# A decode attention that loads the V of two heads as one transfer and runs its loops by pairs of heads

## The chip, the cores and the metric

The kernel runs on one core of a Trainium2 chip. The metric is the device time of one launch in microseconds (us). Before the change it is 2549.87 us, the median of three runs (2549.74 to 2549.97).

## The reference, cut to what matters

Two layers run one after the other; both use the same weights and the same caches. A layer is attention over a cache and then a small mixer with an MLP, for B = 2 sequences of one new token each, D = 576.

```python
def setup():
    B, Sq, D, H, Sk, Dh = 2, 1, 576, 32, 16384, 128
    k_cache, v_cache: (B, H, Sk, Dh) bf16
...
def _A_ref(x, k_cache, v_cache, wq, wo):
    q = (x @ wq) as heads                       # (B, H, 1, Dh)
    scores = einsum("bhqd,bhkd->bhqk", q, k_cache) * Dh ** -0.5
    p = softmax(scores)
    o = einsum("bhqk,bhkd->bhqd", p, v_cache)
    return o as (B, 1, H * Dh) @ wo
...
x = x + _A_ref(layernorm(x), ...)   # layer 0
x = x + _B_ref(layernorm(x), ...)   # w1, w2, w3 (576 x 4608), w4 (4608 x 576)
x = x + _A_ref(layernorm(x), ...)   # layer 1
x = x + _B_ref(layernorm(x), ...)
```

There are U = 2 x 32 = 64 heads a layer. K and V of one head are 16384 x 128 numbers of 2 bytes, 4 MiB each, so a layer reads 512 MiB of cache, and the DMA queue of the whole run moves 1092.40 MB (two heads and a part of a third are kept in memory between the layers).

## The kernel before, in words

**Memory and queue.** `mem` holds NSLOT = 6 slots of TILE = 32768 bytes a partition. One slot holds the K or the V of one head: 128 rows of 32768 bytes, partition p having the keys 128p to 128p + 127. Class `Store` (L269) keeps the list of all transfers of the program in a fixed order (`plan_all`, L499), each with its place in `mem`. A transfer is emitted by `pump` when every cell of its place has been given back by `release`; no later transfer overtakes it. All of them are issued by SP (L101) into one DMA queue, which the 16 DMA engines serve. `used` (L1229) counts what has been read of a tile and releases it after its last reader. `landed` (L1199) puts a relay on POOL, which tells PE, and in the loops DVE too, that a tile has come ("POOLq L202" in the profile).

**Order of tiles.** `tile_order` (L569) alternates K of head s and V of head s - 1. In layer 0 transfer i goes to slot i % 6, in layer 1 to slot (3, 4, 5, 0, 2, 1)[i % 6]. `order` (L565) gives the heads of a layer: 0 to 63 in layer 0, and 62, 63, 61, 0, 1, ..., 60 in layer 1, because the K and V of heads 62 and 63 and parts of head 61 stay in memory over the layers' boundary (CARRY = 2; `park` L1082, `turn`, `settle` and `carried` L1100 do their work there, partly with K already transposed). Head u is sequence u % 2, head u // 2 of it.

**One head** (`attention`, L954). Half of the 128 columns of keys go through PE, half through DVE.
- `q_broadcast` (L1208): DVE copies q's column (`q_col`) and makes `diag` = ident x q (L1213); PE multiplies ones by it (L1217), ACT copies the product (L1220): `qb` holds q in every row.
- PE's half: eight times `transposes` (L1246, 8 blocks of 128x128 into `tps`), `evacuate` by ACT (L1258, `kt`), `scores` (L1272, 8 products of one column into `sps`).
- DVE's half: four times `dots`, a multiply of 128x2048 (L1292) and a sum (L1296) into `s_dve`.
- `softmax_max` (L1299): DVE takes the maxima (L1307, L1310), POOL reduces over the partitions (L1312). `softmax_exp` (L1315): ACT scales (L1321) and takes the exp of both halves (L1324, L1327) into `p`, with the sums in `ls`.
- `pv` (L1348): 128 products of a V block by one column of `p` (L1366), gathered in `mps[:, 448]`. `keep_o` (L1332) and `keep_l` (L1337) store o and the sum on DVE.

Maximum, exp and PV of head s - 1 are interleaved with the transposes of head s: the maximum after its third chunk, the exp after its fifth, PV beside chunks 5 to 8.

**Loops.** PE, ACT and DVE each run real loops whose body holds NS = 3 heads: heads 2 to 61 in layer 0 and positions 4 to 63 of `order(1)` in layer 1, 20 turns each. The heads before and behind them are written out. Within a loop an operation has to have the same buffers in each turn.

**Between the layers.** Behind the loop `totals` (L1164) makes the sums' inverses, the wo, w3, w4 and wq products (L877) follow with weights that come through the same queue, in places that become free one by one. The column of o and l that belongs to a head is given by `place` (L1186); `home` (L1192) copies one column back after layer 1's loop.

Of the kernel before, what the change touches and what calls it, by code (L numbers as in the profile page):

```python
# [328 lines left out]
class KB:  # L329
# [13 lines left out]
    RAW = 2  # L343
    TURNS = {("w3", 0): 1, ("w3", 1): 1, ("w3", 2): 1, ("w4", 1): 1, ("w4", 3): 1, ("w4", 6): 1, ("w4", 8): 1,
# [27 lines left out]
    def _alloc(self):  # L372
# [6 lines left out]
        self.ident = sb("ident", [128, 128], BF16)  # L379
        self.ones_bf = sb("ones_bf", [128, 128], BF16)  # L380
        self.ones_f = sb("ones_f", [128, 128], FP32)
        self.diag = sb("diag", [128, 128], BF16)
        self.qb = [sb(f"qb{i}", [128, 128], BF16) for i in range(self.NS)]
        self.p = [sb(f"p{i}", [128, self.NB], BF16) for i in range(self.NS)]
# [5 lines left out]
        self.l = sb("l", [128, 1 + U], FP32)  # L390
        self.o_acc = sb("o_acc", [128, 1 + U], FP32)
# [15 lines left out]
        self.sel = [sb(f"sel{i}", [128, 128], BF16) for i in range(2)]  # L407
# [18 lines left out]
    def plan_tile(self, t, u, slot, cuts=(), skip=0):  # L426

        b, hh = u % self.B, u // self.B
        src = (self.K if t == "k" else self.V)[b, hh].rearrange("(p j) d -> p (j d)", p=128)
        cuts = [0, *cuts, self.NB]  # L430
        for a, z in zip(cuts[:-1], cuts[1:]):
            if a >= skip:
                self.plan_piece(t, u, slot * self.TILE, src, a, z - a)

# [64 lines left out]
    def plan_all(self):  # L499
# [8 lines left out]
        tiles = self.tile_order(0)  # L508
        place = [i % 6 for i in range(len(tiles))]
        place[-1] = 2  # L510
        half, quarter = self.BP, self.BP // 2
        for (t, u), slot in zip(tiles, place):
            self.plan_tile(t, u, slot, (half, half + quarter) if (t, u) == ("v", U - 1) else ())
        last = {tile: slot for tile, slot in zip(tiles, place)}
        third = U - self.CARRY - 1
        assert last["k", third] == 1 and last["v", third] == 4
# [19 lines left out]
        b, hh = third % self.B, third // self.B  # L536
        tiles = self.tile_order(1)
        b2, h2 = tiles[0][1] % self.B, tiles[0][1] // self.B
        for i in (1, 2, 3, None, 0):
            if i is None:  # L540
                self.plan_piece(*tiles[0], T, self.K[b2, h2].rearrange("(p j) d -> p (j d)", p=128), 0, quarter)
            else:
                self.plan_piece("v", third, 4 * T, self.V[b, hh].rearrange("(p j) d -> p (j d)", p=128),
                                i * self.GONE // 4, self.GONE // 4)
# [921 lines left out]
```

## Time and profile before

| what | value |
| --- | --- |
| median of three runs | 2549.87 us |
| the profiled execution | 2550.04 us |
| its span in the profile | 2548.1 us |
| mean granted clock of TensorE in it | 0.574 |
| instructions | 74895 |
| DVE busy | 1896.9 us |
| ACT busy | 1204.4 us |
| matmuls of PV (L1366) | 16384, 165 ns mean |
| multiplies and sums of DVE (L1292, L1296) | 504 each, 1224 and 2286 ns mean |

The profile is of one execution. Its span goes from the first to the last instruction; the device time of the same execution is 1.9 us longer. Engines are PE (TensorE products), PEld (TensorE weight loads), DVE (VectorE), ACT (ScalarE), POOL (GpSimd) and SP (SyncE, which issues the DMAs here). A row of the timeline gives start and length in us, engine, line, operation, output <- input, shape, and in brackets the idle time ahead of it with what ended it. In the slices of the span each digit is a busy share in tenths, where 9 is 90% or more. A row of DMA issues ends with the median time from issue to landing. "q1" is the queue that SP fills; its packets are single rows of the transfers and small packets of a few bytes.

### The profile page before, as it was taken

The page shows a single profiled execution, that of the slowest core. Times are in us where ns is not written, and L with a number is a line of the kernel's source. Part 1 is how long each engine was busy: PE and PEld are TensorE (multiplying, and loading weights), DVE is VectorE, ACT ScalarE, POOL GpSimd, SP SyncE. Part 2 cuts the span into 40 slices and gives each one's busy share as a digit, 9 for nine tenths or more (in the row PEclk, how much of TensorE's full clock was granted, in tenths as well). Part 3 has the DMA queues.
Part 4 walks back from the last instruction along what each step waited for, and adds up shares of the span by engine and source line. Part 5 has one row for each costly group of instructions (what it writes and reads, how often), then busy time and mean ns, then how long its engine had stood idle before and what let it go on. Part 6 is the DMA issues. An engine that isn't in the chain of part 4 may idle for free.

```text
span 2548.1 us, 74895 instructions
## 1 busy us (share of the span) xinstructions
PE 1614.3 (63%) x34407; PEld 1580.3 (62%) x34407; DVE 1896.9 (74%) x2061; ACT 1204.4 (47%) x1812; POOL 53.5 (2%) x151
## 2 busy tenths in 40 slices
PE   4666666656666666666767766666665666666566
PEld 3666666656665665666667756666665666666566
DVE  5877777777777777777638877777777777777774
ACT  3544544444454444445435544444454445444442
POOL 0000000000000000000000000000000000000000
PEclk8555555555555555555655555555555555555555
DMA  9999999999999999999999999999999999999999
GB/s 411 427 432 432 432 433 431 432 432 432 432 430 433 430 434 431 434 430 434 417 410 430 430 432 431 434 431 431 433 430 434 430 433 430 434 431 434 431 433 386
DMA packets 46928, 1093.19 MB, mean 429 GB/s; under 512 B 5140, under 2 KB 6296, under 8 KB 12440
## 3 DMA queue, kind: packets, MB, share of 16 engines
q1 hardware_dynamic: 46872, 1092.40, 100.0%
q8 instruction: 41, 0.67, 0.1%
q14 instruction: 15, 0.12, 0.0%
HBM read 1092.37 MB, written 0.00 MB: 429 GB/s over the span
## 4 chain that ended last, share of the span: by engine, by line
DMA 66%; DVE 23%; PE 5%; issue 5%; SPq 1%; ACT 0%; DVEq 0%; POOLq 0%
DMA mem<-in_A_k_cache_dram 63%; DVE s_dve L1296 12%; DVE prod L1292 9%; PE tps L1246 2%; PE mps L1366 2%; DMA mem<-in_B_w_dram 1%; DMA mem<-in_A_wo_dram 1%; PE sps L1272 1%; SPq L101 1%; PE sps L1217 1%; DVE diag L1213 0%; DMA mem<-in_A_wq_dram 0%; DVE l L1344 0%; DVE q_col L1210 0%; DVE mx L1307 0%
## 5 line engine op out<-in xcount | busy, mean ns | idle before, releaser
L1258 ACT ACTIVATE kt<-tps 128x1024 bf16<-128x1024 bf16 x992 | 1002.7, 1023 | 878.4 <-PE tps L1246 860.3
L1296 DVE TENSOR_REDUCE s_dve<-prod 128x16 f32<-128x2048 bf16 x504 | 1152.1, 2286 | 17.3
L1246 PE MATMUL tps<-ident,mem 128*128 128x128 bf16 x8192 | 999.4, 300 | 141.6 <-POOLq L202 135.2
L1292 DVE TENSOR_TENSOR prod<-mem,qb 128x2048 bf16<-128x2048 bf16 x504 | 616.8, 1224 | 525.0 <-POOLq L202 493.8
L1366 PE MATMUL mps<-p,mem 128*128 128x1 bf16 x16384 | 512.2, 165 | 549.9 <-POOLq L202 520.0
L1246 PEld LDWEIGHTS tps<-ident,mem 128*128 128x128 bf16 x8192 | 761.1, 136 | 151.6 <-POOLq L202 144.9
L1366 PEld LDWEIGHTS mps<-p,mem 128*128 128x128 bf16 x16384 | 487.6, 104 | 558.4 <-ACT p L1327 552.3
L1272 PEld LDWEIGHTS sps<-q_col,kt 128*128 128x128 bf16 x7936 | 399.1, 113 | 0.6 <-ACT kt L1258 0.5
L1272 PE MATMUL sps<-q_col,kt 128*128 128x1 bf16 x7936 | 387.6, 170 | 0.2
L1217 PE MATMUL sps<-diag,ones_bf 128*128 128x128 bf16 x127 | 36.4, 287 | 195.3 <-DVE diag L1213 195.3
L1217 PEld LDWEIGHTS sps<-diag,ones_bf 128*128 128x128 bf16 x127 | 13.2, 104 | 205.6 <-DVE diag L1213 205.6
L1321 ACT ACTIVATE mx<-mx 128x1 f32<-128x1 f32 x128 | 26.0, 203 | 235.9 <-POOL mx L1312 235.9
L1312 POOL PARTITION_ALL_REDUCE mx<-mx x128 | 51.1, 399 | 2442.2 <-DVE mx L1310 2323.5
L1220 ACT ACTIVATE qb<-sps 128x128 bf16<-128x128 f32 x127 | 35.2, 277 | 137.7 <-PE sps L1217 137.7
L1324 ACT ACTIVATE p<-s_dve,mx 128x64 bf16<-128x64 f32 x126 | 43.8, 348 | 4.1
L1258 ACT ACTIVATE mem<-tps 128x1024 bf16<-128x1024 bf16 x32 | 32.0, 1025 | 21.9 <-PE tps L1246 19.5
L1327 ACT ACTIVATE p<-sps,mx 128x64 bf16<-128x64 f32 x128 | 37.7, 294 | 0.1
L1307 DVE TENSOR_REDUCE mx<-sps 128x1 f32<-128x64 f32 x128 | 27.7, 216 | 7.3 <-PE sps L1272 7.2
L1213 DVE TENSOR_SCALAR diag<-ident,q_f 128x128 bf16<-128x128 bf16 x127 | 31.1, 245 | 0.0
L877 PE MATMUL mps<-prod,mem 128*128 128x2 bf16 x680 | 22.2, 166 | 14.1 <-DMA mem<-in_B_w_dram 8.3
L877 PEld LDWEIGHTS mps<-prod,mem 128*128 128x128 bf16 x680 | 20.6, 104 | 15.9 <-DMA mem<-in_B_w_dram 7.0
L710 ACT ACTIVATE misc<-misc 128x2 f32<-128x2 f32 x8 | 2.4, 296 | 51.8 <-DVE misc L708 51.8
(116 smaller groups left out, 293.7 us busy)
## 6 DMA issues: line engine op xcount, KB each, us to landing
mem<-in_A_k_cache_dram SPq DMA_DIRECT2D x124, 4096.0 KB, 40.7
mem<-in_A_v_cache_dram SPq DMA_DIRECT2D x123, 4096.0 KB, 49.6
mem<-in_B_w_dram SPq DMA_DIRECT2D x21, 576.0 KB, 7.8
mem<-in_B_w_dram SPq DMA_DIRECT2D x7, 1152.0 KB, 33.8
mem<-in_A_v_cache_dram SPq DMA_DIRECT2D x3, 2048.0 KB, 40.4
mem<-in_A_wq_dram SPq DMA_DIRECT2D x10, 512.0 KB, 6.6
mem<-in_A_wo_dram SPq DMA_DIRECT2D x8, 576.0 KB, 19.2
mem<-in_A_wq_dram SPq DMA_DIRECT2D x4, 1024.0 KB, 8.0
```

Source lines behind the costliest of these rows:

```text
L877: ins = pe.matmul(self.mps[:, t * B:(t + 1) * B], lhsT=buf[:, o:o + 128], rhs=rhs(k), start=(k == 0 and t == 0), stop=(k == last), skip_gr ...
L1217: self.pe(lambda pe: pe.matmul(qps, lhsT=self.ones_bf[:, :], rhs=self.diag[:, :], start=True, stop=True, skip_group_check=True), reads=["o ...
L1220: self.act(lambda e: e.activation(out=self.qb[i][:, :], in_=qps, func=ACT.Copy), reads=[("qps", i)], writes=[("qb", i)], sig=("qb", i))
L1246: ins = pe.transpose(self.tps[t][:, j * 128:(j + 1) * 128], buf[:, j * 128:(j + 1) * 128], self.ident[:, :])
L1258: self.act(lambda e: e.activation(out=out, in_=self.tps[t][:, :], func=ACT.Copy), reads=[("tps", t)], writes=keys, sig=("evac", c, t, k))
L1272: ins = pe.matmul(self.sps[sp][:, c * self.CH + j:c * self.CH + j + 1], lhsT=buf[:, j * 128:(j + 1) * 128], rhs=self.q_col[:, sp:sp + 1], ...
L1292: self.dv(lambda e: e.tensor_tensor(out=prod, in0=buf.rearrange("p (j d) -> p j d", d=128), in1=qbc, op=ALU.mult), reads=[("qb", r)] + key ...
L1296: self.dv(lambda e: e.tensor_reduce(out=sd[:, c0:c0 + DB], in_=prod, axis=AX.X, op=ALU.add), reads=["prod"], writes=[("s_dve", r)], sig=(" ...
L1312: self.pool(lambda e: e.partition_all_reduce(mx[3], mx[2], channels=128, reduce_op=ROP.max), reads=[("mx2", i)], writes=[("mx3", i)])
L1324: self.act(lambda e: e.activation(out=p[:, n:self.NB], in_=self.s_dve[i][:, 0:self.NB - n], func=ACT.Exp, bias=mx[4], scale=self.scale, ac ...
L1327: self.act(lambda e: e.activation(out=p[:, 0:n], in_=self.sps[i][:, 0:n], func=ACT.Exp, bias=mx[4], scale=self.scale, accum_out=self.ls[:, ...
L1366: ins = pe.matmul(self.mps[:, 448:449], lhsT=buf[:, j * 128:(j + 1) * 128], rhs=p[:, col:col + 1], start=b == 0, stop=b == self.NB - 1, sk ...
```

## The change

**V by pairs.** Head u now is sequence u // 32, head u % 32 of it, so that heads u and u + 1 lie one behind the other in the cache. In the loops the V of two heads comes as one transfer (`plan_pair`): 8 MiB as 128 rows of 65536 bytes over two slots. Partition p of it has the keys 256p to 256p + 255 of the two heads' 32768 together: the upper 64 partitions hold nothing but the second head, the lower 64 nothing but the first.

**Exp dealt out anew.** The exp of a head lies by K's layout, 128 keys in each of 128 partitions. For the pair, `spread_p` moves it by two products per head with a matrix of ones and zeros into 64 partitions (`both`), 256 columns. The matrix is a window with stride 2 on one tile that now holds ones, ident and the two `sel` matrices side by side (`same`). ACT copies the 64x256 part. `both` has two planes, one a head, and in each plane the other head's 64 partitions stay zero. `pv_pair` then makes 256 products with two columns, so that both heads' o come out at once, in `mps[:, 448:450]`; ACT stores them, and ACT stores the two sums (`keep_pair_l`).

**Loops by two.** A turn has two heads: transfers K, K, pair. The first head's maximum and exp stand in the second head, the second's stand at the end of the turn, with all scores drained before them. PV of both stands behind that. `q_broadcast` of the next head moves between the multiply and the sum of the last `dots` of a head. The loops go from position 1 to 61 (30 turns) in layer 0 and from 4 to 62 (29 turns) in layer 1. The head ahead of each loop is finished by itself first, its PV included; then DVE clears the upper half of `both`'s first plane.

**Places.** Layer 0: K0 in slot 1, V0 in 3, then K in 0 and 2 and the pair in 4 and 5; at the end K61 in 1, K62 in 3, V61 in 4, K63 in 5, V62 in 0, V63 in 2. Layer 1: the rest of its first fresh K in slot 3, its V in 5, then K in 0 and 4 and the pair in 1 and 2; at the end two K in 3 and 5, two V in 0 and 4. The first V after a layer's entry is planned ahead of the second K. The places of layer 1's wo, w3, w4 and w1 change with it.

**Small things.** `ones_f` is one column that is read with stride 0. The sums and o have no extra column, so `home` is gone, and the last product of spread, o and sums is one instruction instead of two.

The diff, cut to its core:

```diff
+    ENTER = (1, 4)
+    LEAVE = (61, 62)
...
-        self.ident = sb("ident", [128, 128], BF16)
-        self.ones_bf = sb("ones_bf", [128, 128], BF16)
+        self.same = sb("same", [128, 4, 128], BF16)
+        self.ones_bf, self.ident, *self.sel = (self.same[:, i, :] for i in range(4))
...
+        both = sb("both", [128, 4 * self.NB], BF16)
+        self.both = both[:, :].rearrange("p (k c) -> p k c", k=2)
...
+    def plan_pair(self, u, slot):
+        v = self.V.rearrange("b h s d -> (b h s d)")
+        n = self.NB * 128 * 128
+        self.store.plan(("w", u, 0, 2 * self.NB), "pair", slot * self.TILE, 2 * self.TILE,
+                        [(lambda m: m, v[u * n:(u + 2) * n].rearrange("(p x) -> p x", p=128))])
...
+        self.plan_tile("k", 0, 1)
+        self.plan_tile("v", 0, 3)
+        for u in range(1, third, 2):
+            self.plan_tile("k", u, 0)
+            self.plan_tile("k", u + 1, 2)
+            self.plan_pair(u, 4)
+        for t, u, slot in (("k", third, 1), ("k", third + 1, 3), ("v", third, 4), ("k", third + 2, 5),
+                           ("v", third + 1, 0), ("v", third + 2, 2)):
...
+        self.plan_tile("k", first, 3, (quarter, half, half + quarter), quarter)
+        self.plan_tile("v", first, 5)
+        for s in range(a, z, 2):
+            self.plan_tile("k", o[s], 0)
+            self.plan_tile("k", o[s + 1], 4)
+            self.plan_pair(o[s], 1)
+        self.plan_tile("k", o[z], 3)
+        self.plan_tile("k", o[z + 1], 5)
+        self.plan_tile("v", o[z], 0)
+        self.plan_tile("v", o[z + 1], 4, (half,))
...
+                                   inside=(lambda: self.q_broadcast(o[s + 1], s + 1)) if turning and c == 2 * n - 2 else None)
...
+                    if odd and c == LEAD:
+                        self.softmax_max(l, s - 1, o[s - 1])
+                    if odd and c == n:
+                        self.softmax_exp(l, s - 1, o[s - 1])
+                        self.spread_p(l, s - 1, 0)
...
+            if turning:
+                if odd:
+                    while pend:
+                        self.scores(*pend.pop(0))
+                    self.softmax_max(l, s, u)
+                    self.softmax_exp(l, s, u)
+                    self.spread_p(l, s, 1)
+                    self.keep_pair_l(l, s - 1)
+                    self.keep_pair_l(l, s)
+                    self.g.relay("tensor", ...)
+                    self.pv_pair(l, s - 1, o[s - 1])
+            elif s == enter - 1:
+                while pend:
+                    self.scores(*pend.pop(0))
+                self.softmax_max(l, s, u)
+                if s - 1 >= 0:
+                    self.keep_o(l, s - 1)
+                    self.keep_l(l, s - 1)
+                self.softmax_exp(l, s, u)
+                self.landed(l, "v", u)
+                for g in range(4):
+                    self.pv(l, s, u, g)
+                self.keep_o(l, s)
+                self.keep_l(l, s)
+                self.dv(lambda e: e.memset(self.both[64:, 0, :], 0.0), writes=self.both_keys)
...
+    def spread_p(self, l, s, k):
+        out = self.sps[0][:, 2 * k * n:2 * (k + 1) * n]
...
+            for h in range(2):
+                at = (1 - k) * 128 + h
+                lhsT = bass.AP(tensor=c.tensor, offset=c.offset + at, ap=[list(c.ap[0]), [2, 128]])
+                ins = pe.matmul(out[:, h * n:(h + 1) * n], lhsT=lhsT, rhs=self.p[i][:, :], start=True, stop=True,
+                                skip_group_check=True)
...
+        lo, hi = 64 * k, 64 * (k + 1)
+        self.act(lambda e: e.activation(out=self.both[lo:hi, k, :], in_=out[lo:hi, :], func=ACT.Copy), ...)
...
+    def pv_pair(self, l, s, u):
...
+                    ins = pe.matmul(self.mps[:, 448:450], lhsT=buf[:, b * 128:(b + 1) * 128], rhs=self.both[:, :, col],
+                                    start=b == 0, stop=b == 2 * self.NB - 1, skip_group_check=True)
...
+        self.act(lambda e, c: e.activation(out=self.o_acc[:, bass.ds(c, 2)], in_=self.mps[:, 448:450], func=ACT.Copy), ...)
+        self.used(l, nm, 2 * self.NB)
```

More of the change, by code (lines that the diff above doesn't have):

```diff
@@ L506, in plan_all @@
         self.plan_small("w2", 0, self.w2, 4 * T + wqr * n + wqr // 2, (0, 64))
-        tiles = self.tile_order(0)
-        place = [i % 6 for i in range(len(tiles))]
-        place[-1] = 2
         half, quarter = self.BP, self.BP // 2
-        for (t, u), slot in zip(tiles, place):
+        third = U - self.CARRY - 1
+        self.plan_tile("k", 0, 1)
[6 more added lines that the diff above has]
+                           ("v", third + 1, 0), ("v", third + 2, 2)):
             self.plan_tile(t, u, slot, (half, half + quarter) if (t, u) == ("v", U - 1) else ())
-        last = {tile: slot for tile, slot in zip(tiles, place)}
-        third = U - self.CARRY - 1
-        assert last["k", third] == 1 and last["v", third] == 4
         self.cuts = {}
```

205 lines of the change are left out of this document (114 added, 91 removed).

## The prediction

> **What bounds the kernel now.** I read the page first: busy shares, the slices, the queue, the chain.
>
> ```profile
> span 2548.1 us, 74895 instructions
> PE 1614.3 (63%) x34407; PEld 1580.3 (62%) x34407; DVE 1896.9 (74%) x2061; ACT 1204.4 (47%) x1812; POOL 53.5 (2%) x151
> ...
> DMA  9999999999999999999999999999999999999999
> GB/s 411 427 432 432 432 433 431 432 432 432 432 430 433 430 434 431 434 430 434 417 410 430 430 432 431 434 431 431 433 430 434 430 433 430 434 431 434 431 433 386
> ...
> q1 hardware_dynamic: 46872, 1092.40, 100.0%
> ...
> DMA 66%; DVE 23%; PE 5%; issue 5%; SPq 1%; ACT 0%; DVEq 0%; POOLq 0%
> ...
> mem<-in_A_k_cache_dram SPq DMA_DIRECT2D x124, 4096.0 KB, 40.7
> mem<-in_A_v_cache_dram SPq DMA_DIRECT2D x123, 4096.0 KB, 49.6
> ```
>
> No engine is busy for more than 74% of the span, while the DMA engines are busy in every slice, at about 432 GB/s wherever K and V stream. A 4 MiB tile is issued 40 to 50 us before it lands, so about four tiles stand in the queue at any time. The time is therefore bytes over rate, plus any moment in which the queue runs dry; there is none now but the ends. An engine's work counts only through the moment at which it frees a slot. So I ask two things: does a byte get cheaper, and does the queue still always hold something? For the second I took the timeline of a steady head.
>
> ```profile
> 617.51 0.25 DVE L1213 TENSOR_SCALAR diag<-ident,q_f 128x128 bf16<-128x128 bf16 x1
> 617.81 0.10 PEld L1217 LDWEIGHTS sps<-diag,ones_bf 128*128 128x128 bf16 x1 [1.58 <-DVE diag L1213]
> ...
> 618.14 0.28 ACT L1220 ACTIVATE qb<-sps 128x128 bf16<-128x128 f32 x1 [0.96 <-PE sps L1217]
> ...
> 622.12 1.22 DVE L1292 TENSOR_TENSOR prod<-mem,qb 128x2048 bf16<-128x2048 bf16 x1 [4.37 <-POOLq L202]
> ...
> 625.70 1.22 DVE L1292 TENSOR_TENSOR prod<-mem,qb 128x2048 bf16<-128x2048 bf16 x1
> ...
> 629.54 0.16 DVE L1310 TENSOR_TENSOR mx<-mx 128x1 f32<-128x1 f32 x1
> ...
> 629.79 0.35 POOL L1312 PARTITION_ALL_REDUCE mx<-mx  x1 [19.08 <-DVE mx L1310]
> ...
> 631.73 0.94 PEld L1366 LDWEIGHTS mps<-p,mem 128*128 128x128 bf16 x32 [5.13 <-ACT p L1327]
> ```
>
> Columns are start, length, engine, line, operation; in brackets the idle time and what ended it. DVE starts at 622.12 after 4.37 us of waiting for a tile: it has slack. A product and its sum take 625.70 - 622.12 = 3.58 us, four of them 14.32. From the last maximum (629.54) over POOL and three ACT steps to the first PV weight load (631.73) it is 2.19 us.
>
> **The change part by part.**
>
> **1. Rows of 65536 bytes.** Two stretches of the DMA view, one of K and V alone, one of weights in long rows:
>
> ```profile
> DMA packets 8599, 250.50 MB, mean 432 GB/s; under 512 B 953, under 2 KB 953, under 8 KB 953
> ...
> q1 hardware_dynamic: 8597, 250.48, 100.4%
> ```
>
> ```profile
> DMA packets 499, 5.11 MB, mean 426 GB/s; under 512 B 59, under 2 KB 59, under 8 KB 59
> ...
> q1 hardware_dynamic: 498, 5.09, 100.4%
> ```
>
> First stretch: 8597 packets of q1, of which 953 are the small ones, so 7644 rows of 32768 bytes (250.48 MB / 7644). In 580 us on 16 engines that is 1214.0 ns a row. A tile is 8 such rows an engine: 9.71 us. Second: 498 - 59 = 439 rows in 12 us, 437.4 ns for 11595 bytes on average. Two points give 0.03668 ns a byte and a fixed 12.1 ns a row. The two layers' loops hold 30 + 29 = 59 pairs; each pair makes 8 rows an engine out of 16. Saving: 59 x 8 x 12.1 ns = **5.7 us**. Ends: 0, if each long row is cut in two again; 8.3 us if the fixed part is 17.6 ns, which the weights stage (below) gives.
>
> ```profile
> DMA packets 5102, 19.85 MB, mean 397 GB/s; under 512 B 569, under 2 KB 569, under 8 KB 5084
> ...
> q1 hardware_dynamic: 5094, 19.73, 100.0%
> ```
>
> Here 5094 - 569 = 4525 rows took 50 us: 176.8 ns for 4360 bytes, and with the 1214.0 this gives 17.6 ns. I take 12.1, from the rows nearest in size. The Trainium skill ("DMA: Bandwidth & Descriptors", section "Where 436 GB/s comes from") puts the ceiling at 435.2 GB/s; by it the fixed part would be 9.3 ns, the saving an estimated 4.4 us and the sum 2562.
>
> **2. A turn of two heads.** Now slots decide. Before, six slots rotate. After, a loop uses four: one for each K, two for the V pair; two stand empty. Let D be the moment at which DVE starts on the first K of a turn. Other durations:
>
> ```profile
> 1253.90 3.57 PE L1366 MATMUL mps<-p,mem 128*128 128x1 bf16 x128 [0.50 <-ACT p L1327]
> ```
>
> ```profile
> 2546.57 0.29 SPq L101 DMA_DIRECT2D out_dram<-prod  x1
> ```
>
> A PV product in a long row of them costs 3.57 / 128 = 27.9 ns. A second column in it I cost at nothing: the weight load sets the pace. An issue needs under 1.5 us to land 2.2 KB (2546.57 to the span's end at 2548.1), so I take 1.4 us to the first byte.
>
> Even head: 14.32 + 0.4 (q_col and diag) = 14.7. Odd head: two products (7.16), the even head's maxima (0.4 by 629.54 + 0.16 against 625.70 + 3.58, taken as 0.5), the third product (3.58), the fourth multiply (1.26), q_col and diag (0.4): PE's q product at D + 27.6. Then last transposes, evacuation, scores, maxima: 3.1 us (next fence: q product 42.23, the first of six evacuations from 43.42 ends at 44.5, then scores and a maximum). Maximum at D + 30.7. The 2.19 us to PE, plus what the new deal of exp adds: two products (0.33, as from 617.81 to its evacuation), an ACT copy of 64x256 (I estimate 0.4, between 0.28 for 128x128 at 618.14 and 1.05 for 128x1024 in the next fence), two semaphores: 1.1. PV starts at D + 34.0, ends 256 x 27.9 ns later at D + 41.1; ACT's copy of two columns, SP's wait: 0.8; first byte of the next pair at **D + 43.3**. In the queue behind this K stand a K, a pair, two K: 5 x 9.71 = 48.55 us after its landing. D is 0.25 us after the landing, so 5.0 us are left. The second K's slot comes free at D + 28.9, first byte D + 30.5, wanted at 38.85: 8 us left. So in steady state the queue does not run dry; the new waits of PE (on exp, on the copy) hold up the next head's transposes behind them, but PE starts that head 3 us late and waits for DVE's diag until D + 12.4 anyway. Cost 0. DVE even loses work (keep_o and keep_l go to ACT). What it costs when this cover is gone stands under the rivals.
>
> **3. Loop entries.** In place of a head that flows into the loop there is now a head that is finished alone: scores drained, maxima, exp, 128 PV products, o and l kept, the memset, and only behind these on DVE the first product of the loop. Layer 0:
>
> ```profile
> 6.86 2.93 SPq L101 DMA_DIRECT2D mem<-in_A_v_cache_dram  x1
> ...
> 42.23 0.10 PEld L1217 LDWEIGHTS sps<-diag,ones_bf 128*128 128x128 bf16 x1 [8.46 <-DVE diag L1213]
> ...
> 43.42 6.31 ACT L1258 ACTIVATE kt<-tps 128x1024 bf16<-128x1024 bf16 x6 [0.58 <-PE tps L1246]
> ...
> 50.70 1.24 POOL L1312 PARTITION_ALL_REDUCE mx<-mx  x1 [35.54 <-DVE mx L1310]
> ...
> 61.52 1.23 DVE L1292 TENSOR_TENSOR prod<-mem,qb 128x2048 bf16<-128x2048 bf16 x1 [3.70 <-issue]
> ```
>
> ```profile
> mem<-in_A_v_cache_dram SPq DMA_DIRECT2D x1, 4096.0 KB, 40.2
> ```
>
> The queue starts K0, V0, K1, K2, all at once as before; the third tile lands at 6.86 + 40.2 = 47.1. The q product at 42.23, maximum at 45.3, 2.19 and 0.9 more because POOL's reduction takes 1.24 here instead of 0.35: PV 48.4 to 52.0; o, l, memset 0.7: 52.7. Then "issue" gaps: 3.70 at this very entry now. I take 2: D = 54.7. The next pair's first byte at 98.0 is wanted at 47.1 + 48.55 = 95.6: **2.4 us** dry (0.4 without a gap, 4.1 with 3.7).
>
> Layer 1:
>
> ```profile
> 1335.22 0.33 SPq L101 DMA_DIRECT2D mem<-in_A_v_cache_dram  x1
> ...
> 1343.05 1.36 POOL L1312 PARTITION_ALL_REDUCE mx<-mx  x1 [17.05 <-DVE mx L1310]
> ...
> 1349.90 1.84 PE L1366 MATMUL mps<-p,mem 128*128 128x1 bf16 x64
> ...
> 1357.60 0.10 PEld L1217 LDWEIGHTS sps<-diag,ones_bf 128*128 128x128 bf16 x1 [2.57 <-DVE diag L1213]
> ...
> 1360.57 0.77 PEld L1246 LDWEIGHTS tps<-ident,mem 128*128 128x128 bf16 x8 [1.71 <-issue]
> ```
>
> ```profile
> mem<-in_A_v_cache_dram SPq DMA_DIRECT2D x1, 4096.0 KB, 15.2
> ```
>
> Behind the rest of K0 come V0 and K1 (before: K1 and V0). The second of them, issued when V62's slot is free, lands at 1335.22 + 15.2 = 1350.4. Then K2, which now goes to slot 4, where V61 lies; its last PV ends at 1349.90 + 1.84 = 1351.7, first byte 1353.3: 2.9 dry. Before, K2 went to the slot of V63, whose PV is done before V61's. The lone head: q product 1357.60, maximum 1360.7, PV 1363.8 (reduction 1.36) to 1367.3, the rest 0.7, gaps 2 (1.71 at this entry now): D = 1370.0, where K1 landed 19.6 us ago. K3's slot is free at D + 13.5, byte 1385.1, wanted at 1382.4: 2.7. K4: D + 30.5 = 1400.5, wanted 1394.8: 5.7. Next pair: D + 43.3 = 1413.3, wanted 1410.2: 3.1. Sum **14.4 us** (12.4 without a gap, 17 with two). One turn later DVE is free before its tile lands again and the 5 us are back.
>
> **4. The rest at nothing.** At either layer's end K61, K62 (K59, K60) now land back to back, which shifts the last maximum by about 1.5 us.
>
> ```profile
> 1258.91 0.16 DVE L1310 TENSOR_TENSOR mx<-mx 128x1 f32<-128x1 f32 x1
> ...
> 1266.18 0.61 PEld L877 LDWEIGHTS mps<-prod,mem 128*128 128x128 bf16 x20 [0.39 <-DMA mem<-in_A_wo_dram]
> ```
>
> ```profile
> 2507.86 0.16 DVE L1310 TENSOR_TENSOR mx<-mx 128x1 f32<-128x1 f32 x1
> ...
> 2519.03 1.41 PEld L877 LDWEIGHTS mps<-prod,mem 128*128 128x128 bf16 x50 [0.68 <-DMA mem<-in_A_wo_dram]
> ```
>
> Behind both maxima the wo products already wait for their DMA (0.39, 0.68), so most hides; 0 to 2.8 us for the two if not. The changed order of q, o and l, the missing copies and one product fewer are under 1 us of DVE.
>
> **Sum.** -5.7 + 2.4 + 14.4 = +11.1 on the profiled run's 2550.04 (span 2548.1 and 1.9 around it); the median, 2549.87, is 0.17 less. **2561 us.**
>
> **Rivals.**
> - *The queue stays fed at the entries* (ends on the other side). Place: the two lone heads. If DVE reached the loop some 14 us sooner in layer 1 than I work out and K2's slot were free in time, only the long rows would count: 2544. It decides from D under 1355.6, where 43.3 us lead to 1398.9. For it: every slice is at full rate today. Against: the multiply-and-sum rows of one head alone run until 1357. Half of the loss gone, 2553, is within 0.2%.
> - *The row is cut again*: no gain, 2567. The packet count decides. Nothing in the trace speaks either way.
> - *The chain of a turn is longer than 5 us over my sum*: strided weights, a slow copy, gaps at each back edge. From D + 48.3 on each further us costs half a us in each of 59 turns (a pair's delay comes back every second turn): 2 us over give 2561 + 59 = 2620. Against: each step has its row, and the rows of a steady head show no such gap.
> - *Long rows move slower.* Their starts lie 64 KiB apart instead of 32. Were the pairs' 495 MB to go at the weights stage's 397 GB/s instead of 432, it would be +101: 2662. No row hints at it. The Trainium skill ("DMA: Bandwidth & Descriptors", section "Latency and other measured facts") has row pitches of large powers of two slow down, but first at 512 KiB; no run here shows it.
>
> **How the numbers follow.** Forecast 0.70, the cut row 0.13, the long chain 0.05, slow rows 0.02, fed entries 0.05, half of the loss 0.05. A measurement of this kernel can tell about 0.2% (5.1 us) from no change. Slower by more than that: 0.70 + 0.13 + 0.05 + 0.02, less 0.03 for the forecast's own lower edge, 0.87; same 0.05 + 0.03 = 0.08; faster 0.05. Range: the forecast's own ends are -8.3 + 0.4 + 12.4 = +4.5 (2554) and 0 + 4.1 + 17 + 2.8 = +23.9 (2574), the cut row lies inside; 2 us more on either side take in part of the half case and one more gap: 2552 to 2576.
>
> **What would show it.** q1 packets 46872 - 59 x 144 = 38376 (45928 if cut). DMA share under 1 around 1350 to 1415, and a little near 96; full elsewhere. K's median from issue to landing falls from 40.7 to between 20 and 26, and still nothing waits in the loops except DVE for a tile. I am wrong if the loops show DMA below 432, or if DVE begins layer 1's loop before 1360.

## The result, and the profile after

The changed kernel takes 2565.85 us (median of four runs, 2564.69 to 2569.81) against 2549.89 before: a ratio of 1.0065, with an interval of 1.0048 to 1.0083. It is slower by 16.0 us; 11.1 were forecast, in a range of 2552 to 2576. The profiled execution is the longest of the four, 2569.81 us with a span of 2567.9, so the stages below add up to 19.8 us and not to 16.0.

First the page of the changed kernel: span, slices, queue, the chain's shares, and the rows of K's DMA issues.

```profile
span 2567.9 us, 75499 instructions
PE 1590.8 (62%) x34642; PEld 1525.9 (59%) x34642; DVE 1876.3 (73%) x1821; ACT 1251.0 (49%) x2106; POOL 106.3 (4%) x152
...
DMA  9999999999999999999998999999999999999999
GB/s 413 382 435 438 426 440 425 433 434 431 433 438 426 432 435 429 432 436 429 398 401 362 410 426 432 432 440 425 440 426 432 433 436 427 439 427 433 435 430 394
...
q1 hardware_dynamic: 38376, 1092.39, 99.1%
...
DMA 59%; DVE 26%; PE 7%; issue 6%; ACT 1%; SPq 0%; POOL 0%; POOLq 0%; DVEq 0%; ACTq 0%
...
mem<-in_A_k_cache_dram SPq DMA_DIRECT2D x124, 4096.0 KB, 23.2
```

No engine is much busier than before, and the same bytes come in 38376 packets: the long rows are moved whole. The loss is in three places of the GB/s row: slice 2 (382), slices 20 and 21 (398, 401, where the kernel before has 417 and 410) and slices 22 and 23 (362, 410). K's issue to landing fell from 40.7 to 23.2 us. The queue that held about four tiles now holds two or three (23.2 us at 9.7 us a tile), so a slot that comes free late is felt sooner.

How much each stage costs can be read from the bytes. The next fences give what q1 has moved up to 140, 1180, 1340, 1500 and 2500 us, first before, then after (packets, MB, share of 16 engines).

```profile
q1 hardware_dynamic: 3149, 58.63, 98.7%
...
q1 hardware_dynamic: 18565, 507.69, 100.1%
...
q1 hardware_dynamic: 26565, 574.18, 100.1%
...
q1 hardware_dynamic: 28917, 642.83, 100.1%
...
q1 hardware_dynamic: 43812, 1074.41, 100.2%
```

```profile
q1 hardware_dynamic: 2761, 55.88, 94.7%
...
q1 hardware_dynamic: 14332, 505.82, 99.6%
...
q1 hardware_dynamic: 22119, 570.54, 99.5%
...
q1 hardware_dynamic: 23813, 632.90, 98.6%
...
q1 hardware_dynamic: 34938, 1065.58, 99.3%
```

The difference of two such rows over 0.432 MB a us is how far the changed kernel is behind at that moment: 2.75 MB at 140 us are 6.4 us. Rows that are on their way make an error of about 1 us, an estimate: 16 rows of 32768 bytes, one on each engine, are 1.2 us at this rate.

| stage | forecast, us | behind at its end, us | its own share, us |
| --- | --- | --- | --- |
| start and entry, layer 0 (to 140) | +2.4 | 6.4 | +6.4 |
| loop, layer 0 (to 1180) | -2.9 | 4.3 | -2.0 |
| layers' boundary (to 1340) | 0 | 8.4 | +4.1 |
| entry, layer 1 (to 1500) | +14.4 | 23.0 | +14.6 |
| loop, layer 1 (to 2500) | -2.8 | 20.4 | -2.5 |
| end | 0 | 19.8 (span) | -0.6 |

The two loop forecasts are the 5.7 us by their 30 and 29 pairs. Layer 1's entry and the loops came out near their forecasts; layer 0's entry and the layers' boundary were taken too small.

This execution is also worse than most in just these two. The second experiment below has the same kernel up to 1340 us, and its profiled execution took 2565.86 us, which is the median of the change. It is 4.5 us behind at 140 us, 2.9 at 1180 and 4.9 at 1340, so layer 0's entry and the boundary cost 4.5 and 2.1 us there instead of 6.4 and 4.1. The fourth experiment's profile gives 4.5 and 2.3.

A steady turn first, from the timeline of the changed kernel: DVE's first product of two turns running, and SP's issue of the next pair.

```profile
597.93 1.23 DVE L1344 TENSOR_TENSOR prod<-mem,qb 128x2048 bf16<-128x2048 bf16 x1 [8.60 <-POOLq L202]
...
636.71 1.23 DVE L1344 TENSOR_TENSOR prod<-mem,qb 128x2048 bf16<-128x2048 bf16 x1 [8.74 <-POOLq L202]
...
637.64 0.33 SPq L101 DMA_DIRECT2D mem<-in_A_v_cache_dram  x1
```

A turn takes 38.8 us, four tiles at 9.7. DVE stands 8.7 us of it for its tile, and the pair's slot is free at D + 39.7 (D: DVE's start on a turn's first K) where the prediction had D + 41.9 (its first byte at D + 43.3). Nothing is dry here. Now the entry of layer 0:

```profile
50.59 0.17 DVE L1077 MEMSET both<- 64x128 uint32 x1
...
57.39 1.23 DVE L1344 TENSOR_TENSOR prod<-mem,qb 128x2048 bf16<-128x2048 bf16 x1 [6.64 <-issue]
...
99.03 0.33 PE L1439 MATMUL mps<-both,mem 128*128 128x2 bf16 x7 [2.30 <-issue]
...
99.67 0.33 SPq L101 DMA_DIRECT2D mem<-in_A_v_cache_dram  x1
```

DVE is done with the lone head at 50.76 and begins the loop at 57.39: 6.64 us in which it waits for nothing that the profile shows ("issue"). PE stands 2.30 us in the same way within the first turn's PV. In the profiles of experiments 1, 2 and 4, with the same entry, these gaps are 5.43 to 5.54 and 1.61 to 1.79 us, which is about the 1.9 us by which their entry is cheaper. The queue's view of the same moments has the packets of the instruction queues, once from 50 to 58 us and once from 96 to 99.5:

```profile
q1 hardware_dynamic: 99, 3.60, 106.0%
q8 instruction: 1, 0.02, 0.9%
q14 instruction: 3, 0.02, 0.8%
```

```profile
q1 hardware_dynamic: 31, 0.49, 33.6%
q8 instruction: 1, 0.02, 1.7%
```

Ten packets of the instruction queues lie between 50 and 140 us, and only 3 in the 1040 us of the loop behind them, so code is loaded mostly there. But four of the ten lie between 58 and 96 us, where the timeline shows no such gap. The Trainium skill ("Runtime: NRT & Kernel Launch", section "Instruction fetch mechanics") says that an engine's code comes in pages over a DMA queue of its own and that a taken branch to a page that isn't there stalls the engine. The rows agree in place, with 6.64 and 2.30 us; that it is the cause was not isolated by a run.

Layer 1's entry (the second of the two transfers from 1341.27 on is K2):

```profile
1341.27 20.17 SPq L101 DMA_DIRECT2D mem<-in_A_k_cache_dram  x2
...
1359.24 1.84 PE L1465 MATMUL mps<-p,mem 128*128 128x1 bf16 x64
1361.48 0.43 SPq L101 DMA_DIRECT2D mem<-in_A_v_cache_dram  x1
...
1375.86 1.23 DVE L1344 TENSOR_TENSOR prod<-mem,qb 128x2048 bf16<-128x2048 bf16 x1 [0.26 <-issue]
...
1379.87 2.48 PEld L1294 LDWEIGHTS tps<-same,mem 128*128 128x128 bf16 x24 [4.85 <-issue]
...
1388.99 15.64 SPq L101 DMA_DIRECT2D mem<-in_A_k_cache_dram  x2
...
1418.02 0.33 PE L1439 MATMUL mps<-both,mem 128*128 128x2 bf16 x7 [2.83 <-issue]
...
1418.66 0.33 SPq L101 DMA_DIRECT2D mem<-in_A_v_cache_dram  x1
```

V61's last PV ends at 1361.08; only then does K2 go out, and the pair at once behind it. DVE begins the loop at 1375.86. 1370.0 was forecast on the clock of before; the changed kernel enters this stage 8.4 us behind that, so D is 2.5 us earlier than forecast, about the 2 us of gap that are 0.26 here. The next pair goes out 42.8 us later. The slices of 1340 to 1440 us show the dry places, one digit for each 2.5 us:

```profile
DMA  9999993065999999999969996099990919999996
```

They lie around 1355 to 1365, 1400 to 1405 and 1415 to 1422 us: in front of K2, of K4 and of the next pair. In front of K3, for which 2.7 us were forecast, one digit falls to 6 (1390 to 1392.5 us), which is about 1 us.

### The profile page after: what moved, and what is told of

Read it like the earlier page. It is cut to its first block, busy times and chain, and to the rows that moved or that the text cites. A ratio compares the mean times of both kernels' runs of the same rounds, so it can differ in the third digit from the quotient of the medians.

```text
span 2567.9 us, 75499 instructions
## 1 busy us (share of the span) xinstructions
PE 1590.8 (62%) x34642; PEld 1525.9 (59%) x34642; DVE 1876.3 (73%) x1821; ACT 1251.0 (49%) x2106; POOL 106.3 (4%) x152
## 3 DMA queue, kind: packets, MB, share of 16 engines
q1 hardware_dynamic: 38376, 1092.39, 99.1%
## 4 chain that ended last, share of the span: by engine, by line
DMA 59%; DVE 26%; PE 7%; issue 6%; ACT 1%; SPq 0%; POOL 0%; POOLq 0%; DVEq 0%; ACTq 0%
DMA mem<-in_A_k_cache_dram 56%; DVE s_dve L1350 17%; DVE prod L1344 9%; PE tps L1294 3%; DMA mem<-in_B_w_dram 1%; PE mps L1465 1%; PE sps L1324 1%; PE mps L1439 1%; PE sps L1265 1%; DMA mem<-in_A_wq_dram 1%; ACT mem L1310 0%; SPq L101 0%; DVE diag L1261 0%; DVE q_col L1258 0%; POOL mx L1366 0%
## 5 line engine op out<-in xcount | busy, mean ns | idle before, releaser
L1310 ACT ACTIVATE kt<-tps 128x1024 bf16<-128x1024 bf16 x992 | 966.8, 1028 | 188.8 <-PE tps L1294 174.3
L1294 PE MATMUL tps<-same,mem 128*128 128x128 bf16 x8192 | 915.0, 286 | 28.2 <-issue 22.3
L1294 PEld LDWEIGHTS tps<-same,mem 128*128 128x128 bf16 x8192 | 735.4, 131 | 34.1 <-issue 27.5
L1439 PEld LDWEIGHTS mps<-both,mem 128*128 128x128 bf16 x15104 | 407.6, 103 | 48.6 <-ACT both L1419 43.3
L1439 PE MATMUL mps<-both,mem 128*128 128x2 bf16 x15104 | 412.6, 165 | 32.9 <-ACT both L1419 27.8
L1324 PEld LDWEIGHTS sps<-q_col,kt 128*128 128x128 bf16 x7936 | 353.1, 108 | 66.3 <-ACT kt L1310 64.6
L1413 PE MATMUL sps<-p,same 128*128 128x128 bf16 x236 | 46.6, 301 | 483.0 <-ACT p L1381 483.0
L1265 PE MATMUL sps<-diag,same 128*128 128x128 bf16 x126 | 36.0, 285 | 316.7 <-DVE diag L1261 311.4
L1366 POOL PARTITION_ALL_REDUCE mx<-mx x128 | 103.8, 811 | 2412.9 <-DVE mx L1364 2306.1
L1419 ACT ACTIVATE both<-sps 64x256 bf16<-64x256 f32 x118 | 44.5, 378 | 57.5 <-PE sps L1413 57.5
L1378 ACT ACTIVATE p<-s_dve,mx 128x64 bf16<-128x64 f32 x123 | 42.8, 348 | 4.0
## 6 DMA issues: line engine op xcount, KB each, us to landing
mem<-in_A_k_cache_dram SPq DMA_DIRECT2D x124, 4096.0 KB, 23.2
```

Of the source, the lines that this page charges most:

```text
L1265: self.pe(lambda pe: pe.matmul(qps, lhsT=self.ones_bf[:, :], rhs=self.diag[:, :], start=True, stop=True, skip_group_check=True), reads=["o ...
L1294: ins = pe.transpose(self.tps[t][:, j * 128:(j + 1) * 128], buf[:, j * 128:(j + 1) * 128], self.ident[:, :])
L1310: self.act(lambda e: e.activation(out=out, in_=self.tps[t][:, :], func=ACT.Copy), reads=[("tps", t)], writes=keys, sig=("evac", c, t, k))
L1324: ins = pe.matmul(self.sps[sp][:, c * self.CH + j:c * self.CH + j + 1], lhsT=buf[:, j * 128:(j + 1) * 128], rhs=self.q_col[:, sp:sp + 1], ...
L1366: self.pool(lambda e: e.partition_all_reduce(mx[3], mx[2], channels=128, reduce_op=ROP.max), reads=[("mx2", i)], writes=[("mx3", i)])
L1378: self.act(lambda e: e.activation(out=p[:, n:self.NB], in_=self.s_dve[i][:, 0:self.NB - n], func=ACT.Exp, bias=mx[4], scale=self.scale, ac ...
```

## The experiments

The theory at this point: the long rows are worth some 10 ns each; the rest is lost at the entries, where only the moment D counts at which DVE starts on the loop's first K, because the pair's slot comes free 43 us behind it. The rival: each late slot has a price of its own. By its interval the change costs 12 to 21 us, so what a run saves or loses against it by a few us is read from the stages' bytes, too, and not from the medians alone.

**1. The rows.** The pair's V in two transfers of 32768-byte rows, all else alike:

```diff
-                        [(lambda m: m, v[u * n:(u + 2) * n].rearrange("(p x) -> p x", p=128))])
+                        [(lambda m, h=h: m[:, h * self.TILE // 2:(h + 1) * self.TILE // 2],
+                          v[u * n:(u + 2) * n].rearrange("(p x) -> p x", p=128)[:, h * self.TILE // 2:(h + 1) * self.TILE // 2])
+                         for h in range(2)])
```

> The changed kernel with one thing undone: the pair's V comes in two transfers of 128 rows of 32768 bytes each instead of one of 65536-byte rows; places, loops and waits stay. The changed kernel is at 2565.9 us (2564.7 to 2569.8). Theory (the long rows are worth some 10 ns a row, 59 x 8 x 10 ns = 4.8 us, and the losses lie at the entries and the layers' boundary): 2570.7, between 2569 and 2573, q1 packets 45928. Rival (the rows are worth nothing, what looks like a gain in the loops is the queue's catching up): 2566. Rival (long rows are slower): below 2565.

Measured: 2570.1 us (2568.7 to 2572.0), 4.2 above the change, in 46872 packets where 45928 were expected. Its rows of q1 at 140, 1180, 1500 and 2500 us:

```profile
q1 hardware_dynamic: 3088, 56.67, 96.1%
...
q1 hardware_dynamic: 18498, 505.50, 99.8%
...
q1 hardware_dynamic: 28603, 633.59, 98.9%
...
q1 hardware_dynamic: 43426, 1065.32, 99.4%
```

It is 4.5, 5.1, 21.4 and 21.0 us behind the kernel before: through the loops it neither gains nor loses (+0.5, -0.3), where the long rows gain 2.0 and 2.5. So the gain is the rows', not the queue's catching up. The runs of the two kernels overlap; the tenth experiment repeats this with eleven runs a side that don't.

**2. The order of K2 and the pair.** In layer 1's first turn the pair is queued first:

```diff
+            if s == a:
+                self.plan_pair(o[s], 1)
             self.plan_tile("k", o[s + 1], 4)
-            self.plan_pair(o[s], 1)
+            if s > a:
+                self.plan_pair(o[s], 1)
```

> The changed kernel, but in the first turn of layer 1 the V pair is queued ahead of the second K, so that nothing waits for the slot of V61 first. Theory (only the moment D at which DVE starts on the loop's first K counts: the next pair's slot is free 43 us behind it, and whatever was dry before is paid out of the same loss): no change, 2565.9 within 1.5 us; the dry place of 4.8 us in front of the second K is gone or moved, the ones behind it grow by as much. Rival (each wait of a K for its slot is a cost of its own): 4 to 5 us less, 2561.

Measured: 2568.0 us (2565.9 to 2569.8), no gain; it is 2.2 above the change, where at most 1.5 were expected, with runs that overlap. From its timeline, and then its slices of 1340 to 1440 us:

```profile
1354.64 0.33 SPq L101 DMA_DIRECT2D mem<-in_A_v_cache_dram  x1
1356.50 45.57 SPq L101 DMA_DIRECT2D mem<-in_A_k_cache_dram  x3
...
1371.79 1.23 DVE L1347 TENSOR_TENSOR prod<-mem,qb 128x2048 bf16<-128x2048 bf16 x1 [0.26 <-issue]
...
1414.93 0.33 SPq L101 DMA_DIRECT2D mem<-in_A_v_cache_dram  x1
```

```profile
DMA  9999819999999999998999500999909999999989
```

The pair is out at 1354.6 and K2 at 1356.5, and yet the second pair goes out 43.1 us after D, as it did (42.8). The two runs come into this stage 4.9 and 8.4 us behind; counted from there the first pair is out 3.3 us earlier than in the change, and the second only 0.2. The dry place in front of K2 shrinks by these digits from 6.5 to some 2.7 us, the one in front of K4 grows from 3.5 to 6.2, and the stage costs 13.5 us instead of 14.6, a difference within the error. So the dry place in front of K2 was worth little or nothing. These dry moments are not a sum of independent prices; the last of them decides.

**3. DVE off the lone head.**

```diff
-                self.keep_o(l, s)
-                self.keep_l(l, s)
-                self.dv(lambda e: e.memset(self.both[64:, 0, :], 0.0), writes=self.both_keys)
+                self.act(lambda e, c: e.activation(out=self.o_acc[:, bass.ds(c, 1)], in_=self.mps[:, 448:449], func=ACT.Copy),
+                         reads=["ops"], writes=["o_acc"], col=self.place(l, s))
+                self.keep_pair_l(l, s)
+                self.act(lambda e: e.activation(out=self.both[64:, 0, :], in_=self.both[64:, 0, :], func=ACT.Copy, scale=0.0),
+                         reads=self.both_keys, writes=self.both_keys)
```

> The changed kernel, but the three operations of DVE behind the lone head's PV (o, l, the clearing of both) are made by ACT, in both layers; DVE goes from the lone head's maximum straight to the loop. Theory (DVE's start in the loop sets the loss): D falls by 5.2 us in layer 0 (57.39 to some 52) and by 5.7 in layer 1 (1375.9 to some 1370.2, or less where DVE stands for its code), and the time by 5 to 10 us: 2558, between 2555 and 2561. Rival (PE's drain at the lone head, not DVE, holds the loop back): under 2 us, 2564 to 2566.

Measured: 2558.8 us (2556.1 to 2559.5), 7.1 less than the change.

```profile
51.80 1.23 DVE L1346 TENSOR_TENSOR prod<-mem,qb 128x2048 bf16<-128x2048 bf16 x1 [6.51 <-issue]
...
1363.68 1.23 DVE L1346 TENSOR_TENSOR prod<-mem,qb 128x2048 bf16<-128x2048 bf16 x1 [0.42 <-POOLq L202]
...
1380.97 1.23 DVE L1346 TENSOR_TENSOR prod<-mem,qb 128x2048 bf16<-128x2048 bf16 x1 [2.91 <-ACT qb L1270]
...
1408.22 0.33 SPq L101 DMA_DIRECT2D mem<-in_A_v_cache_dram  x1
```

DVE's start in layer 0 moved from 57.39 to 51.80, and at 140 us q1 has moved 58.67 MB, as much as before the change: the loss at layer 0's entry is gone, to the error of 1 us. The "issue" gap is still there (6.51 us); DVE only comes to it sooner. In layer 1 10.0 us remain of 14.6 (4.82 MB short at 1500 us, 0.49 at 1340). There PE is late in turn: DVE stands 2.91 us for the next q, and the pair goes out 44.5 instead of 42.8 us after D.

**4. Layer 1 enters two heads later**, with V by itself until then:

```diff
-    ENTER = (1, 4)
+    ENTER = (1, 6)
...
+        for t, i, slot in (("k", 4, 0), ("k", 5, 2), ("v", 4, 1), ("v", 5, 3)):
+            self.plan_tile(t, o[i], slot)
...
-                elif s > leave:
+                elif s > leave or 0 < s < enter:
...
+                    if s < enter:
+                        if c == n:
+                            self.softmax_exp(l, s - 1, o[s - 1])
+                            self.landed(l, "v", o[s - 1])
+                        if 0 <= c - n < 4:
+                            self.pv(l, s - 1, o[s - 1], c - n)
```

> The changed kernel, but layer 1 enters its loop two heads later (28 pairs instead of 29); these two heads run in the way of before, K and V by themselves in the slots that are free then (K in 0 and 2, V in 1 and 3). Theory (the entry's loss is DVE's lag behind the tiles, 17.5 us at the first K of the loop; two heads of 14.3 us of DVE beside 19.4 us of DMA give back 10 us of it): layer 1's entry loses some 5 instead of 14.6 us, 2557, between 2554 and 2560. Rival (the lone head's drain costs the same wherever it stands): 2565.

Measured: 2559.5 us (2558.3 to 2561.1), 6.4 less than the change. Layer 1's entry costs 6.2 us instead of 14.6 (4.82 MB short at 1500 us, 2.16 at 1340). So the drain does not cost the same wherever it stands, as the rival had it: DVE's lag was the cost, and two heads give back most of it.

**5. Both edits together.**

> The edits of the third and the fourth run together: three operations behind each lone head's PV go from DVE to ACT, and layer 1 enters its loop two heads later. Theory (only DVE's start on the loop's first K counts): layer 0 gains the 5.3 us that the third run's trace shows there, and in layer 1 the loop starts 5.7 us sooner than in the fourth, of which some 2 are lost because PE is then late with the next head's q product (2.9 us in the third run): 2559.5 - 5.3 - 3.5 = 2550.7, between 2548 and 2553. Rival (what the two save in layer 1 is the same time): 2554.

Measured: 2553.0 us (2550.1 to 2555.2), nearer to the rival's 2554 than to the 2550.7. The 5.3 us of layer 0 came (5.0 at 140 us). Of the 3.5 hoped for in layer 1 only 0.7 did (its entry costs 5.5): the expectation had PE's lateness too small.

```profile
1394.51 1.23 DVE L1354 TENSOR_TENSOR prod<-mem,qb 128x2048 bf16<-128x2048 bf16 x1 [0.42 <-POOLq L202]
...
1406.09 2.74 PE L1304 MATMUL tps<-same,mem 128*128 128x128 bf16 x24 [6.47 <-issue]
...
1413.89 1.23 DVE L1354 TENSOR_TENSOR prod<-mem,qb 128x2048 bf16<-128x2048 bf16 x1 [4.99 <-ACT qb L1278]
...
1441.02 0.33 SPq L101 DMA_DIRECT2D mem<-in_A_v_cache_dram  x1
```

DVE is in the loop at 1394.51, but PE gets to the loop's first transposes only at 1406.09, after 6.47 us of "issue"; then DVE stands 4.99 us for q. The pair goes out 46.5 us after D. "Only D counts" is thus too simple: from the point at which DVE no longer is the last, PE's entry counts.

**6. K61 ahead of the last pair of layer 0.** At the boundary K61 lands behind the last pair's two tiles, and the first wo goes out at 1246.04 instead of 1236.22; 4.3 of these 9.8 us the queue was behind already. In the changed kernel:

```profile
1218.77 1.22 DVE L1344 TENSOR_TENSOR prod<-mem,qb 128x2048 bf16<-128x2048 bf16 x1 [8.46 <-DMA mem<-in_A_k_cache_dram]
...
1241.39 0.16 DVE L1364 TENSOR_TENSOR mx<-mx 128x1 f32<-128x1 f32 x1
...
1246.04 30.68 SPq L101 DMA_DIRECT2D mem<-in_A_wo_dram  x8
```

```diff
+            if u + 2 == third:
+                self.plan_tile("k", third, 1)
             self.plan_pair(u, 4)
-        for t, u, slot in (("k", third, 1), ("k", third + 1, 3), ("v", third, 4), ("k", third + 2, 5),
+        for t, u, slot in (("k", third + 1, 3), ("v", third, 4), ("k", third + 2, 5),
```

> The run before, and in layer 0 K61 is queued ahead of the last V pair; its slot stands empty all through the loop. Theory (at the layers' boundary the queue is dry for some 2.5 us since DVE stands 8.5 us for K61, which comes two tiles later than a K by itself did, so that V61's place is free late for wo): 2.5 us less than the run before, 2548.2; the loss between 545 and 550 MB of the queue goes from 2.5 us to under 0.5. Rival (the boundary's loss comes from the pair's late PV): no change or worse, as the pair lands 9.7 us later.

Measured: 2553.1 us (2550.8 to 2556.3), no change from the fifth, to which the edit was added. The boundary costs 1.4 instead of 1.8 us: the rival held. V61 has to wait for the slot of the pair, which now lands later, and goes out at 1220.31 instead of 1213.91. Between 1260 and 1270 us, where the queue ran dry for wo, the fifth loses 2.2 us and the sixth 0.2; between 1210 and 1230, ahead of V61, they lose 0.8 and 2.1.

**7 and 8. Later entries.** Layer 1 at its ninth head, then layer 0 at its fourth too; the two lines that say it (the tiles of the heads between are planned as in 4):

```diff
-    ENTER = (1, 6)
+    ENTER = (1, 8)
...
-    ENTER = (1, 8)
+    ENTER = (3, 8)
```

> The run before, but layer 1 enters its loop at its ninth head (27 pairs), and the loop's K slots change places. Theory (the lag of DVE is used up by then: it would be free 1429 us from the start, the loop's first K lands at 1436): the loop starts with its tile, nothing is dry behind it, 3 us less than the run before, 2545.2. Rival (the lone head's drain costs PE some us wherever it stands): no change.

> The run before, but layer 0 too enters its loop two heads later (29 pairs). Theory: the first K of the loop lands at 86 us, when DVE has just become free; what is left of layer 0's loss (1.0 us in the third run's trace) goes: 2544.3. That is the time of before less 4.5 us for the long rows and 1.4 at the end. Rival (one pair less and more code by the instruction queues cost as much): no change from the run before.

Measured: 2550.6 (2549.3 to 2551.6) and 2549.6 us (2548.4 to 2552.3). In the seventh, layer 1's entry costs 1.2 us (0.75 MB short at 1500 us, 0.23 at 1340). The seventh's gain of 2.5 and the eighth's of 1.0 are about the 3.0 and 0.9 expected, though the eighth's runs overlap with the seventh's; their totals are 5 us above what was hoped, as the fifth and sixth had brought 5 less.

**9, 10, 11. The places.** Layer 0's loop in slots 0, 5 and 2-3, so that K61 and V61 find empty slots, with the other places of both layers to match; the tenth is the ninth with the rows cut as in 1; the eleventh moves V1 and V2.

```diff
-            self.plan_tile("k", u + 1, 2)
+            self.plan_tile("k", u + 1, 5)
...
-            self.plan_pair(u, 4)
+            self.plan_pair(u, 2)
...
-        for t, u, slot in (("k", third + 1, 3), ("v", third, 4), ("k", third + 2, 5),
-                           ("v", third + 1, 0), ("v", third + 2, 2)):
+        for t, u, slot in (("k", third + 1, 0), ("v", third, 4), ("k", third + 2, 5),
+                           ("v", third + 1, 2), ("v", third + 2, 3)):
```

> The run before with other places: in layer 0 the loop's K go to slots 0 and 5 and the pair to 2 and 3, so that K61 and V61 both find empty slots behind the loop and neither waits for the last pair's PV; the places of layer 1 follow from it. Theory (what is left of the loss at the layers' boundary, 2.9 us between 520 and 550 MB of the queue, is the wait of V61 for the last pair's slot and of wo for V61's): 2.5 us less than the run before, 2547.1, and 0.1% under the kernel before the change. Rival (the boundary's loss has another cause, the late PV itself): no change, 2549.6.

> The run with other places, and the pair's V in two transfers of 32768-byte rows as in the first run. Theory (57 pairs of 8 rows at some 10 ns, in a kernel whose queue is hardly dry): 4.6 us more than the run with other places, 2551.7. Rival (the long rows are worth nothing): the same time.

> The run with other places, with two places of layer 0's start mended: V1 goes to slot 3 and V2 to slot 1, which are empty early, where V2 had to wait for V0's slot (its transfer was issued at 65.5 us, and the queue was dry for 2 us). Theory: 2 us less than the run with other places, 2549.0, 0.9 us under the kernel before the change, which is within 0.2%. Rival (another wait takes its place): 2551.

Measured: 2551.0 (2549.5 to 2553.3), 2555.4 (2554.5 to 2556.4) and 2549.6 us (2548.5 to 2550.4). The ninth missed its total. Its boundary costs 0.5 us where the eighth's costs 2.6, but V2 waited for V0's slot and cost some 1.4 us by 140 us, which the eleventh gave back: 2549.56. The tenth, 4.4 above the ninth, gives the worth of the long rows a second time, and here the eleven runs of either lie apart. These kernels have 56 pairs (38808 packets are 56 x 144 fewer than before), not the 57 of the expectation. The eighth and the eleventh differ by 3 us in their profiles at 2500 us (1074.05 and 1075.36 MB) and not in their medians (2549.63 and 2549.56); the runs of each lie 2 to 4 us apart, those of the kernel before beside the eighth too (2549.34 to 2552.56), and why was not found.

The best version stands at 0.9998 of the kernel before, interval 0.9989 to 1.0007: the change's loss is gone, but it doesn't beat the kernel before by what can be told apart.

## Why the prediction was right, point by point

- **The sign and the size.** +16.0 measured, +11.1 forecast, by the mechanism forecast: the loops gain a little, the entries lose more.
- **Rows of 65536 bytes.** Forecast 5.7 us at 12.1 ns a row. The first experiment gives 4.2 us over 59 x 8 rows, 8.9 ns; the tenth 4.4 over 56 x 8, 9.8 ns. The nearest rows of the trace were mixed sizes with a mean of 11595 bytes, and the line through them puts the fixed part too high. The row is not cut: 38376 packets, as forecast for that case. The 4.4 us that the prediction estimated with the Trainium skill ("DMA: Bandwidth & Descriptors", section "Where 436 GB/s comes from") agree with the 4.2 and 4.4.
- **A turn of two heads.** No dry moment, as forecast; the second column of PV costs nothing (256 products from 630.33 to 637.32 in the steady turn, 27.3 ns each, where one column took 27.9). The reason that the prediction gives, the weight load, no run isolates.
- **Layer 0's entry.** Too small: 2.4 us forecast, 6.4 found here and 4.5 in the profiles of experiments 1, 2 and 4. The failing step is 'Then "issue" gaps: 3.70 at this very entry now. I take 2': the gap of DVE was 6.64 us, and the 2.30 us of PE within the first PV were not in the sum. Part of it was hidden, since DVE was done with the lone head at 50.76 and not at 52.7; POOL's reduction took 0.38 us there, not the 1.24 taken from before. The next pair went out at 99.67 instead of 96.6, and the queue also thinned out at 72 to 75 and at 82 to 90 us, which the prediction does not name. The third experiment removed the loss by starting DVE earlier.
- **Layer 1's entry.** 14.4 forecast, 14.6 found, but not by its items: K2's wait was longer, K3's shorter, DVE's gap was 0.26 instead of 2 us and PE's 4.85 and 2.83. The items are chained: each wanted time is counted from the tile before with its delay, so their sum is that of the last wait alone. The second experiment bears this out, by cutting the first item for next to nothing. That this last wait came within 0.2 us is luck, too: D was 2.5 us earlier than forecast, but the queue also ran out some 3 us earlier (at about 1356 us, 8.4 of it lag, where the forecast has 1350.4).
- **"The rest at nothing."** Wrong in layer 0: 4.1 us at the boundary in this profile and 1.8 to 2.3 in those of experiments 1 to 4, where the prediction had 0 and as the end of the range 2.8 for both layers. The step that failed is "Behind both maxima the wo products already wait for their DMA (0.39, 0.68), so most hides". It priced the last maximum, which came 2 us later beyond the lag. But the first wo goes to V61's place, and V61's products wait for the exp of head 61. That head's maximum came at 1241.39 instead of 1231.73, 5.4 us later beyond the 4.3 of lag, and wo with it; the short waits for wo were a sign of a queue with nothing to spare. In the ninth and eleventh experiments, with empty slots for K61 and V61, the boundary costs 0.5 us. There V61 no longer waits (it goes out at 1187.54 in the eleventh, at 1219.63 in the eighth), which accounts for about half of the 2.1 us between the two; wo itself goes out no earlier (1238.33 and 1238.41), and the rest was not traced.
- **The rivals.** The queue that stays fed needed D under 1355.6; D was 1375.86. The cut row and the slow rows fall by the packets and by the first experiment, the long chain by the steady turn, D + 39.7.

Of the 3.9 us between the profiled execution and the median of the change, 3.5 are there by 1340 us, at layer 0's entry and the boundary, if the second experiment's profile is taken for the median. Why the "issue" gaps are longer in one execution than in another stays open.

## What to carry to other kernels

In a kernel bound by its DMA queue, larger transfers trade slack for size. Here the bytes got 4 us cheaper, and the places that had to be empty together left less in the queue wherever the loop begins or ends. Price such a change at its entries and exits, not in its loop, and follow there the last wait alone; the waits before it are paid out of the same loss. Leave room for up to several us of "issue" where an engine enters a loop, on whichever engine is last.

## What the hardware showed unexpectedly

- An engine that entered a loop stood 0.26 to 6.64 us under "issue", DVE in some runs and PE in others (6.47 in the fifth), with packets of the instruction queues in the same stretch. The size was not predictable from the row of the kernel before (3.70).
- POOL's reduction over the partitions took 399 ns on average before and 811 after. In the steady turn the first head's takes 1.25 us and the second's 0.35:

```profile
620.13 1.25 POOL L1366 PARTITION_ALL_REDUCE mx<-mx  x1 [30.35 <-DVE mx L1364]
628.06 0.35 POOL L1366 PARTITION_ALL_REDUCE mx<-mx  x1 [6.68 <-DVE mx L1364]
```

  The long one follows 30.35 us of idle time, the short one 6.68; but at layer 0's entry one took 0.38 us after 29.86, so idle time alone is not the reason. In the steady turn it lies off the path, and why it is longer was not tried.
- The mean granted clock of TensorE was 0.570 to 0.575 in the runs of the kernel before and 0.612 to 0.621 in those of the change and of every experiment, with PE busy for 63% and 62% of the span. Nothing here tells why, and in the loops the time does not hang on PE.
